# Softmax attention beside linear attention on one core: the last unit's normalisation, the range check, the head and the planner's keys are changed

## The chip, the cores and the metric

The kernel runs on one core of a Trainium2 chip. A core has a matrix engine (TensorE, PE in the profile), a vector engine (VectorE, DVE), an activation engine (ScalarE, ACT), a general engine (GpSimd, POOL), a queue engine that issues DMAs (SyncE, SP), an on-chip memory (SBUF) of 128 partitions and an accumulator memory (PSUM) of eight banks[...]. The metric is device time in microseconds (us), as the median of several executions.

## The reference: two attention layers whose outputs stand side by side

```python
qkv = (x @ wqkv).reshape(B, S, 3, H, Dh)          # B=1, S=2048, D=512, H=32, Dh=16; both layers
# A: softmax attention
p = softmax(einsum("bhqd,bhkd->bhqk", q, k) * Dh**-0.5)
a = einsum("bhqk,bhkd->bhqd", p, v).reshape(B, S, D) @ wo
# B: linear attention with a learned feature map
phi(t) = concat(softmax(t @ w_phi), softmax(-(t @ w_phi)))     # 32 features per head
kv = einsum("bhsf,bhsd->bhfd", phi(k), v);  z = phi(k).sum(over s)
b = (einsum(phi(q), kv) / (einsum(phi(q), z) + 1e-6)).reshape(B, S, D) @ wo
out = concatenate([a, b], axis=-1)                # [1, 2048, 1024], bf16
```

Nearly all the work is A's: 32 heads with a score matrix of 2048 x 2048 each.

## The kernel before

**A's tiling.** The work is cut into 32 units: a unit is a group g of four heads (eight groups, lined up two to a block of 128 projected columns, with a mask `hmask` that keeps every other head of the block in the key copy) and a chunk c of 512 queries. Each unit has 16 key tiles of 128 keys. For a key tile, PE makes four score blocks of 128 x 512 (`kq`, L654), one per head. They become exponentials in one of two ways. ACT applies exp to two or three blocks at once (L795, into `pT`). Or DVE makes them: it converts scores to 16-bit patterns that are read as floats (L852, into `rg`), and adds three shifts to the result (L873); the four versions are multiplied with four scaled copies of V, so the sum approximates exp. Of the 16 key tiles, five (`DK`) may go to DVE. PE multiplies all of them with V (L661) and collects a unit in one PSUM bank. V is stored as `VP` with 17 columns per head, the 17th being one, so that the row sums come along. PE also runs matmuls by zero (`filler`, L688) where its recent activity would fall too low.

**The end of a unit** (`make_unit_end`). DVE copies the bank to SBUF (`X`, L708). A DMA collects the row sums in `sums` (L714), DVE inverts them (L717), a DMA writes the inverses to HBM (`scr`, L720), four DMAs spread them over the partitions of `Yd` (L723), and POOL multiplies X by Yd in two halves (L730), into `OT` for an even group, into `Oo` for an odd one, from which four DMAs move it to its partitions of OT (L737). `X`, `Yd` and `Oo` have two buffers each. When the eight groups of a chunk are done, `out_proj` multiplies OT by wo (L918), DVE copies each of four row tiles to `OA` (L922), and a DMA stores it (L926).

**B** runs beneath A in steps that are released as A advances (`b_steps`): after its loads and the folding of w_phi into the weights, sixteen k-steps (L1002 to L1044) and sixteen q-steps. A q-step makes numerators and denominators on PE (L1078), divides by the feature sums on DVE (L1088, L1091), adds and normalises on POOL and DVE (L1105 to L1115), transposes on PE (L1121), copies the transposed tile on ACT (L1124), multiplies by wo (L1127), copies on DVE (L1131) and stores (L1134). Most of its buffers are double.

**The range check.** All this is valid only where sums lie in a range. After everything else, three DVE instructions count over `sums` and `rmin` (L1162 to L1166), two more combine the counts, a tiny matmul adds over partitions and DVE writes `flag` (L1172). A second program (`_general`) follows in the code; each engine loads the flag and skips it if the range holds.

**The order.** A planner (`_Sched`) writes each engine's instruction list when the program is built; on the chip each engine runs its list in order and waits on semaphores. Tasks stand in streams, one or more per engine, each with a weight from `_W`. `_choose` (L219) gives the head of each stream the start that the planner expects, adds the weight, and takes the lowest sum:

```python
st = self._start(t, r)
w = s["w"]
cand.append([st, st + (w(t) if callable(w) else w), s, r])
```

Here r is when the task's inputs and buffers are ready. The stream of score blocks for ACT, `pe_qa`, is `urgent`: other PE tasks that would delay it are charged `guard`. POOL's tasks wait for the last DVE task marked `port`. `b0`, `b1`, `b2` are the shares of A's key tiles at which B's k-steps begin, its q-steps begin, and they end; `p0`, `p1`, `p2` place the later Q and K projections; `cut` and `lead` say near the end of a unit when DVE may still take a tile.

**The head.** PE runs 16 warm-up matmuls (L536), then transposes the first 512 rows of x (L542). Copies of these go to `xT`; the first K projection, then the first Q projection follow (L581), then V row by row (L578).

## Time and profile before

The median of 14 executions is 798.89 us (794.47 to 801.3). The profiled execution took 800.21 us.

| | us |
|---|---|
| span of the profile | 798.4 |
| first exp on ACT starts | 12.60 |
| last exp on ACT ends | 760.48 |
| last copy of a B row tile (L1131) ends | 788.01 |
| last A row tile copied (L922) | 785.66 |
| flag written (L1172) ends | 790.38 |
| ACT busy | 752.3 |
| DVE busy | 722.1 |
| PE busy | 730.0 |

A line of the groups of instructions reads: line, engine, operation, output<-input, shapes, count | busy us, mean ns of one | idle us of the engine just before them, and what ended most of it. Mean durations overlap with the neighbours, so busy time divided by the count is what one costs in a row of them. A line of the stretches reads: from:to, its length, then busy us and number of instructions for each engine, then the granted PE clock (1 is full), the share of the DMA engines, and GB/s. The chain of waits gives start, length and instruction.

### The profile page before, as it was taken

To read this page: it belongs to the slowest core of one execution; us is meant where nothing else is said; L and a number is where in the kernel's file an instruction comes from. 1 tells how busy PE (TensorE), PEld (TensorE's weight loads), DVE (VectorE), ACT (ScalarE), POOL (GpSimd) and SP (SyncE) were. 2 spreads that over 40 slices of the span, in tenths; PEclk is the share of its full clock that TensorE was granted. 3 is DMA by queue.
4 is the path that set the end of the run, shared out by engine and by line. 5 is a ranking of instruction groups with operands and counts; after the bars stand their busy time and mean duration, and the time that the engine had idled before them with its cause. 6 is when DMAs were issued, how large, how long until landed. Compare 5 with 4: busy or idle time off the path is not lost.

```text
span 798.4 us, 17735 instructions
## 1 busy us (share of the span) xinstructions
PE 730.0 (91%) x7368; PEld 221.5 (28%) x7429; DVE 722.1 (90%) x1278; ACT 752.3 (94%) x819; POOL 157.5 (20%) x233
## 2 busy tenths in 40 slices
PE   8999999999998999899999899989999999999964
PEld 3322222232222232222222222222222222233331
DVE  1788999999998999999998989899999999978973
ACT  5999999999999999999998999999999999999930
POOL 5221111110003110000012322101103000164462
PEclk9999999999999999999997999999999999999987
DMA  7200000280000000000010000000000000000111
GB/s 146 66 9 8 7 6 13 50 183 8 13 32 15 9 4 11 9 12 9 18 29 9 12 2 12 9 9 12 9 25 20 20 10 12 8 15 18 28 44 52
DMA packets 44155, 19.62 MB, mean 25 GB/s; under 512 B 33312, under 2 KB 42016, under 8 KB 44064
## 3 DMA queue, kind: packets, MB, share of 16 engines
q1 hardware_dynamic: 42480, 17.60, 9.3%
q8 instruction: 60, 0.98, 0.5%
q10 hardware_dynamic: 1584, 0.79, 0.5%
q14 instruction: 31, 0.25, 0.1%
HBM read 7.88 MB, written 4.46 MB: 15 GB/s over the span
## 4 chain that ended last, share of the span: by engine, by line
ACT 83%; PE 11%; DVE 3%; issue 1%; DMA 0%; POOL 0%; DVEq 0%; ACTq 0%; POOLq 0%
ACT pT L795 78%; PE PS L654 3%; PE PS L661 3%; ACT e_k L1005 2%; PE PS L581 1%; ACT eT L1068 1%; DVE rg L852 1%; PE PS L536 1%; PE PS L1127 1%; ACT e_k L1124 1%; PE PS L578 1%; DVE rg L873 1%; PE PS L918 1%; ACT Wf L1068 0%; DMA out_dram<-e_k 0%
## 5 line engine op out<-in xcount | busy, mean ns | idle before, releaser
L795 ACT ACTIVATE pT<-PS 128x1024 bf16<-128x1024 f32 (+2 forms) x721 | 708.5, 1149 | 4.5 <-PE PS L654 4.3
L852 DVE TENSOR_SCALAR rg<-PS 128x512 uint16<-128x512 f32 x516 | 332.3, 683 | 17.8 <-PE PS L654 15.3
L654 PE MATMUL PS<-QT,KT 32*128 32x512 bf16 x2048 | 308.3, 387 | 31.9 <-ACT pT L795 26.7
L873 DVE TENSOR_SCALAR rg<-rg 128x2048 uint16<-128x2048 uint16 x387 | 251.8, 694 | 3.5 <-PE PS L661 3.0
L654 PEld LDWEIGHTS PS<-QT,KT 32*128 32x128 bf16 x2048 | 78.5, 91 | 292.1 <-ACT pT L795 230.3
L661 PE MATMUL PS<-pT,VP 128*32 128x512 bf16 x1532 | 153.1, 392 | 5.7 <-ACT pT L795 3.6
L661 PE MATMUL PS<-rg,VJ 128*32 128x512 f16 x1548 | 142.7, 388 | 0.4
L661 PEld LDWEIGHTS PS<-pT,VP 128*32 128x32 bf16 x1532 | 39.2, 93 | 97.8 <-issue 57.7
L730 POOL TENSOR_TENSOR Oo<-X,Yd 128x256 bf16<-128x256 f32 x32 | 22.8, 729 | 176.0 <-DVE rg L873 118.5
L730 POOL TENSOR_TENSOR OT<-X,Yd 128x256 bf16<-128x256 f32 x32 | 22.8, 728 | 171.6 <-DVE rg L873 136.8
L1015 POOL TENSOR_TENSOR w<-e_k,stat 128x512 bf16<-128x512 bf16 x32 | 33.7, 1073 | 100.7 <-DVE rg L873 46.8
L661 PEld LDWEIGHTS PS<-rg,VJ 128*32 128x32 bf16 x1548 | 39.2, 95 | 48.8 <-DVE rg L873 22.1
L661 PE MATMUL PS<-rg,VP 128*32 128x512 f16 x516 | 50.8, 384 | 0.2 <-DVE rg L852 0.2
L688 PE MATMUL PS<-ones_t,zer 128*32 128x512 bf16 x504 | 47.2, 388 | 0.0
L581 PE MATMUL PS<-xT,w 128*128 128x512 bf16 x114 | 34.0, 382 | 3.0 <-issue 1.9
L1105 POOL TENSOR_TENSOR w<-w 128x272 f32<-128x272 f32 x32 | 23.9, 762 | 41.7 <-DVE rg L873 29.6
L1124 ACT ACTIVATE e_k<-PS 128x512 bf16<-128x512 bf16 x16 | 10.3, 641 | 20.5 <-PE PS L1121 20.4
L708 DVE COPY X<-PS 128x512 f32<-128x512 f32 x32 | 21.9, 685 | 5.7 <-PE PS L661 5.6
L1091 DVE TENSOR_TENSOR w<-PS,stat 128x408 f32<-128x408 f32 (+1 forms) x48 | 25.2, 525 | 1.0
L1115 POOL TENSOR_TENSOR w<-w,den 128x256 bf16<-128x256 f32 x32 | 19.4, 622 | 28.0 <-DVE den L1111 9.4
L1127 PE MATMUL PS<-woB,e_k 128*128 128x512 bf16 x58 | 18.1, 415 | 2.9 <-ACT e_k L1124 1.0
L1008 DVE TENSOR_REDUCE stat<-e_k 128x64 f32<-128x1024 bf16 x16 | 19.5, 1216 | 0.7 <-ACT e_k L1005 0.4
(85 smaller groups left out, 425.0 us busy)
## 6 DMA issues: line engine op xcount, KB each, us to landing
Yd<-scr SPq DMA_DIRECT2D x128, 32.0 KB, 1.8
out_dram<-OA SPq DMA_DIRECT2D x16, 128.0 KB, 1.7
out_dram<-e_k SPq DMA_DIRECT2D x16, 128.0 KB, 1.7
OT<-Oo SPq DMA_DIRECT2D x64, 16.0 KB, 1.8
w<-in_A_wqkv_dram SPq DMA_DIRECT2D x2, 384.0 KB, 4.0
OT<-in_A_x_dram SPq DMA_DIRECT2D x1, 512.0 KB, 4.7
w<-in_A_wqkv_dram ACTq DMA_DIRECT2D x1, 512.0 KB, 7.9
WOp<-in_A_wo_dram SPq DMA_DIRECT2D x1, 512.0 KB, 6.4
```

The costliest lines, as they stand in the source:

```text
L581: return e.matmul(bank_of(t), w[:, ct, c0:c0 + 128], xT[:, ct, c * 512:(c + 1) * 512], start=(ct == 0), stop=(ct == 3))
L654: return e.matmul(out_ap, KT[32 * r:32 * r + n, g, kt * 128:(kt + 1) * 128], QT[32 * r:32 * r + n, c, g // 2, :], start=True, stop=True, t ...
L661: return e.matmul(PS[32 * r:32 * r + 32, pvb[u].idx, :], lhs(8 * (g // 2) + 2 * r + g % 2), rhs(r), start=t.res["first"], stop=t.res["last ...
L688: P.op("pe", lambda e, r=r: e.matmul(PS[32 * r:32 * r + 32, pvb[u].idx, :], zer[:], ones_t[:].unsqueeze(1).broadcast_to([128, 4, 128]), st ...
L730: ms.append(put(po_n, _Task("pool", 0.7, one("pool", lambda e, t, cs=cs: e.tensor_tensor(OT[:, c % 2, g // 2, cs] if even else Oo[:, ms[0] ...
L795: return e.activation(pT[:, p:p + n, :].rearrange("p a n -> p (a n)"), PS[:, b:b + n, :].rearrange("p a n -> p (a n)"), ACT.Exp, scale=0.25)
L852: return e.tensor_scalar(rg[:, q0.res["i"].idx, 512 * r:512 * r + 512], PS[:, qk.res["D"].idx, :], ya, yb, ALU.mult, ALU.add)
L873: ad = put(dv_ad, _Task("dve", 0.59, one("dve", lambda e, t, j=j: e.tensor_scalar(rg[:, t.res["j"].idx, :], rg[:, q0.res["i"].idx, :], flo ...
L1015: ph.append(put(po_phi, _Task("pool", 1.03, one("pool", lambda e, t, a=a: e.tensor_tensor(pk[ph[0].res["k"].idx][:, 512 * a:512 * a + 512] ...
L1091: muls.append(put(dv_y, _Task("dve", 0.485, one("dve", lambda e, t, yv=yv, lo=lo, n=n: e.tensor_tensor(ysv[r0.res["y"].idx][:, 136 * lo:13 ...
L1105: ad = [put(po_y, _Task("pool", 0.73, one("pool", lambda e, t, k=k: e.tensor_tensor(y3(0)[:, 2 * k:2 * k + 2], y3(0)[:, 2 * k:2 * k + 2], ...
L1127: o1, o2 = two_step(pe_o, lambda e, t, i: e.matmul(bank_of(t), oT_b[tp.res["t"].idx][:, i, :], woB[:, i, :], start=(i == 0), stop=(i == 3) ...
```

## The change

- **Last unit.** `last_unit` replaces the way over HBM for unit 31: PE multiplies X by a selection matrix `sel` in fp32, so that each head's row sums stand in all its partitions; DVE inverts them in four pieces of 128 columns from PSUM and multiplies each by X into `Oo`. The out-projection of the last chunk takes OT without the last odd group against `WOp` and `WOl[:, 0]`, and a fifth product of Oo against `WOl[:, 1]` is added per row tile; `WOl` is the last block of wo, with every other head's rows zeroed, made by POOL. The last row tile is copied by ACT. Unit 30 is multiplied by DVE in one piece.
- **All other units.** One DMA instead of four fills all partitions of Yd.
- **Range check.** It becomes planned tasks with two streams of their own (`dv_ck`, `pe_ck`), released at the last unit's X.
- **Head.** Q is projected first; K's first 128 keys are projected and copied alone, then the other 384 (`first_k`); 12 warm-ups instead of 16.
- **Planner.** A task's key falls by 0.03 per us that it has been ready; many weights, and b0, p1, p2, `cut`, are new.
- **B's oT copy** (L1124) goes to DVE. `VP` loses 16 spare columns, and its column of ones is filled in one instruction.

```diff
-                    cand.append([st, st + (w(t) if callable(w) else w), s, r])
+                    cand.append([st, st + (w(t) if callable(w) else w) - _W["age"] * (st - r), s, r])
...
-          dred=-0.1, dv=-0.081, dkv=-0.118, dy=-0.011, dd=-0.058, dob=-0.124, dmn=0.059, akf=-0.155,
-          aqf=-0.077, aot=-0.365, spare=9, early=0.0, guard=0.346, cut=4, lead=6, b0=0.315, b1=0.54, b2=0.99,
-          p0=8, p1=22, p2=5.753, lone=0, psh=0, pn=4, ps=-0.308, el=2, both=0)
+          dred=-0.076, dv=-0.053, dkv=-0.118, dy=-0.02, dd=0.003, dob=-0.124, dmn=0.059, akf=-0.019,
+          aqf=-0.072, aot=-0.365, age=0.03, early=0.0, guard=0.346, cut=5, lead=6, b0=0.286, b1=0.54, b2=0.99,
+          p0=8, p1=30, p2=6.012, psh=0, pn=1, ps=-0.308, el=2, both=0, va=16, ka=8, ota=0, xlat=3.6)
...
-    for i in range(16):
+    for i in range(12):
...
+    def first_k():
+        for lo, hi in ((0, 128), (128, 512)):
+            t0 = put(pe_pj, _Task("pe", 0.24 if hi == 128 else 0.65, pe_group(4, lambda e, t, ct, lo=lo, hi=hi: e.matmul(
+                PS[:, t.res["b"].idx, lo:hi], w[:, ct, 512:640], xT[:, ct, lo:hi], start=(ct == 0), stop=(ct == 3))),
+                [l_k0, xt_ready[(0, 0)], xt_ready[(0, 1)]], lat=PL, need=[("b", G, 1, 2)]))
...
-    proj("k", 0, 0, True)
     proj("q", 0, 0)
+    first_k()
...
+            if u == NU - 1:
+                col.append(d1)
+                last_unit(xv, xi, c)
+                range_check(xv, d1)
+                return
...
-            d3 = put(sp_q, _Task("sp", 2.0, dma(lambda t: d_s3[t.res["y"].idx], lambda e, t, r: e.dma_start(
-                Yd[32 * r + 16 * (g % 2):32 * r + 16 * (g % 2) + 16, t.res["y"].idx, :],
-                scr[u][r:r + 1, :].broadcast_to([16, 512])), 4), [d2], lat=2.2, need=[("y", y_sl, 1, 2)]))
+            d3 = put(sp_q, _Task("sp", 0.6, dma(lambda t: d_s3[t.res["y"].idx], lambda e, t, i: e.dma_start(
+                Yd[:, t.res["y"].idx, :], scr[u].unsqueeze(1).broadcast_to([4, 32, 512]))), [d2], lat=2.6,
+                need=[("y", y_sl, 1, 2)]))
...
+    def last_unit(xv, xi, c):
+        bc = put(pe_op, _Task("pe", 0.9, pe_group(1, lambda e, t, i: e.matmul(
+            PS[:, t.res["b"].idx, :], sel[:], X[:, xi, :], start=True, stop=True)), [xv], lat=PL, pre=[t_sel],
+            need=[("b", G, 1, 4)]))
+        parts = []
+        for k in range(4):
+            cs = slice(128 * k, 128 * k + 128)
+            r = put(dv_n, _Task("dve", 0.98, one("dve", lambda e, t, cs=cs: e.reciprocal(
+                Yd[:, parts[0][0].res["y"].idx if parts else t.res["y"].idx, cs], PS[:, bc.res["b"].idx, cs])), [bc], lat=DL,
...
+            m = put(dv_n, _Task("dve", 0.22, one("dve", lambda e, t, cs=cs: e.tensor_tensor(
...
-            te = put(ac_ot, _Task("act", 0.49, one("act", lambda e, t: e.activation(
...
+                te = put(dv_ot, _Task("dve", 0.35, one("dve", lambda e, t: e.tensor_copy(
...
-    c0 = P.op("dve", lambda e: e.tensor_scalar(
-        junk, sums[:], _A_LO, None, ALU.is_ge, ALU.add, accum_out=cnt[:, 0:1]), c_deps)
```

## The prediction

> **What bounds the kernel now.** I read the engine shares first, then the busy time in five stretches, then the chain of waits from the last exp to the end, then the groups of instructions behind each step.
>
> ```profile
> span 798.4 us, 17735 instructions
> PE 730.0 (91%) x7368; PEld 221.5 (28%) x7429; DVE 722.1 (90%) x1278; ACT 752.3 (94%) x819; POOL 157.5 (20%) x233
> ```
>
> Three engines look full. The stretches tell them apart:
>
> ```profile
> core 0: us, PE busy (x) PEld busy (x) DVE busy (x) ACT busy (x) POOL busy (x), PEclk, DMA share, GB/s
> 0.00:12.60 12.60, 10.62 (x49) 4.49 (x51) 2.46 (x4) 4.07 (x5) 9.66 (x28) 1.00 0.90 177
> 12.60:760.50 747.90, 699.46 (x7209) 208.28 (x7267) 698.89 (x1220) 742.72 (x806) 132.50 (x180) 0.99 0.09 21
> 760.50:788.40 27.90, 19.78 (x111) 8.69 (x110) 19.16 (x46) 5.53 (x10) 15.30 (x26) 0.82 0.19 60
> 788.40:790.40 2.00, 0.16 (x1) 0.08 (x1) 1.59 (x9) 0.00 (x0) 0.00 (x0) 1.00 0.21 70
> 790.40:798.40 8.00, 0.00 (x0) 0.00 (x0) 0.00 (x0) 0.00 (x0) 0.00 (x0) 0.59 0.05 13
> ```
>
> From the first exp (12.60) to the last (760.48) ACT is busy 742.7 of 747.9: ACT sets the pace. Then comes a tail of 28 us in which ACT does almost nothing, DVE works 19.2, the range check alone takes 2, and 8 us follow in which no engine works. Head, tail and check are 50 us without exps.
>
> ```profile
> L795 ACT ACTIVATE pT<-PS 128x1024 bf16<-128x1024 f32 (+2 forms) x721 | 708.5, 1149 | 4.5 <-PE PS L654 4.3
> L852 DVE TENSOR_SCALAR rg<-PS 128x512 uint16<-128x512 f32 x516 | 332.3, 683 | 17.8 <-PE PS L654 15.3
> L873 DVE TENSOR_SCALAR rg<-rg 128x2048 uint16<-128x2048 uint16 x387 | 251.8, 694 | 3.5 <-PE PS L661 3.0
> ```
>
> These are the attention tiles. DVE makes 516/4 = 129 of the 512 key tiles at (332.3+251.8)/129 = 4.53 us each, ACT the other 383 at 708.5/383 = 1.85 us. Together they make 1/1.85 + 1/4.53 = 0.761 tiles per us: an engine's us freed or lost is converted with these rates.
>
> The tail, by the chain of waits (start, length, what):
>
> ```profile
> 761.76 0.69 DVE X L708
> ...
> 764.11 3.44 DMA out_dram<-e_k
> ...
> 777.81 1.89 PE PS L1127 x4
> 779.70 4.03 PE PS L918 x14
> 783.74 0.05 issue
> 783.79 0.38 PE PS L918
> 784.17 0.24 PE PS L1121 x4
> 784.43 0.61 ACT e_k L1124
> ```
>
> Two chains share it. A's last unit: X copied at 762.45, its multiply on POOL at 772.00, out-projection L918 at 779.5, last A copy L922 done at 785.66. B's q-steps: eight of the sixteen casts L1131 fall after 763, the last ends at 788.01. They hold each other up: transposes L1121 of B stand behind L918 on PE, and out_dram<-e_k behind the last unit's DMAs on SP. B is late because it was starved: POOL's L1115 is busy 0.9 us in 617 to 697 and 6.2 us in 697 to 730, while DVE's L852 fills the first stretch.
>
> **What the Trainium skill says.** "FP8 and Floating Point Precision", TensorE Precision Notes: a true FP32 matmul takes four passes. No fp32 matmul is in this trace; four warm 512-column passes at the 0.216 us spacing seen here give an estimate of 0.86 us. "TensorE: Matmul & The Clock Gate", Part 1: the clock is released by a busy window of about 3.4 us that runs freely; Part 4: transposes do not count as busy. The trace agrees so far: warm-up matmuls come 0.43 us apart until about 6.6 us, then at half that. "SBUF — State Buffer", Summary: a DVE instruction in a two-port mode, or with two SBUF inputs against POOL's reads, blocks POOL for its length. POOL's longest waits here are for L873, 137 and 119 us before L730.
>
> **The change part by part.** The sum is made in span; the profiled run took 800.21 (span 798.4 plus 1.8), 1.3 above the median 798.89, from which I subtract.
>
> *Head.* Four warm-ups fewer at 0.43 us: the queue would empty at 6.2, the transposes start at 7.12 now, and x has landed at 0.79 + 4.7 = 5.5, so 0.9 us gain. If the clock is still low, 16 transposes at twice 0.055 lose 0.9 and eight projection matmuls at 0.21 more lose 1.7: a loss of 1.7 is the other end. I take 0. Q before K, and K for 128 keys alone: today Q's cast ends at 11.88 and ACT takes two K copies (10.39 to 11.65) and a V copy before the exp at 12.60. With Q's four matmuls first (9.3 to 10.2), four of 128 columns (0.25) and a short K copy, the exp can start at about 11.4: 1.2 gained; two more copies on ACT lose about 0.4. The V load (issued 1.9, lands after 7.9) covers the V matmuls from 10 on. POOL's ones (8.2 us, becoming one strided fill), the 16 columns less of VP and two WOl multiplies stay under POOL's first awaited work at 17.5 and its 80% idle. **Head −1.0 (−2.5 to +1.5).**
>
> *oT copy from ACT to DVE.* Ten of sixteen L1124 lie in the body, 0.49 us each in the chain: ACT gains 4.9. On DVE I take 0.40 (L556 copies twice the elements from PSUM in 0.69; bounds 0.35 and 0.69): DVE loses 4.0. That is 4.9/1.85 − 4.0/4.53 = 1.77 tiles, or **−2.3** (−1.4 to −2.6).
>
> *Range check.* Now L1162 to L1172, ending at 790.38, 2.0 after the last output issue on SP (788.37). Done earlier on DVE, **−2.0**; its 1.8 us of DVE work go into the tail below. Uncovered it costs all 2.0 again.
>
> *Last unit.* Removed: one small reciprocal, 1 + 4 + 4 DMAs (their issues on SP: 1.17, 1.71 and 2.47 us), and two POOL multiplies. Added: one fp32 matmul (0.9, twice that at the low clock), four reciprocals of 128 columns from PSUM (L1088: 295 ns for 24 columns, 235 for 16, so about 7 ns each more: 1.0 us; L1011's 547 for 64 says 0.95) and four multiplies (272 columns take 426, so 0.3): 5.2 us on DVE. A's chain from X (762.45) becomes 1.1 + 0.2 + 5.2, the last product and copy 1.1, issue 0.35: 10 us after the last exp against 25.5 now. The first three products per row tile are ahead of it. The single Yd DMA of the other units shortens SP's issue from 1.7 to about 0.5 and doubles the bytes to 256 KB; a unit lasts 23 us and X has two buffers, so it is hidden.
>
> *The tail as a sum.* DVE's 19.2 us hold X 0.69, a reciprocal 0.24 and four A copies 2.75; 15.5 are B. After, with B as late as now: 15.5 + six oT copies 2.4 + X 0.7 + three A copies 2.1 + chain 5.2 + check 1.8 = 27.7, which fills today's 27.9. So removing DMAs alone brings nothing: DVE is late next. The gain must come from B's backlog.
>
> *Age and the new weights.* Each us that a ready task waits lowers its key by 0.03. A B multiply (about −0.02) passes an A conversion (−0.165) after 5 us; today it never does while conversions are ready. Raising the A adds from 0.031 to 0.113 and starting k-steps at 0.286 instead of 0.315 (22 us) push the same way. One us of B on DVE moved into the body costs 0.221/0.761 = 0.29 us there and gives 1/0.9 in the tail (nine tenths packed). I take 12 of the 17.9 us (B with its oT copies): the tail is 15.7/0.9 = 17.4, −10.5 + 3.5 = **−7.0**. Bounds: all but 2 moved, a tail of 13 us (A's own 10 and some waits), −10.2; none moved, 27.7/0.9 = 30.8, +2.9.
>
> Sum: −1.0 − 2.3 − 2.0 − 7.0 = −12.3; 798.89 − 12.3 = **786.6**. That is 780 to 793 within this case.
>
> **The rivals.**
> *Backlog stays, DVE bounds the tail.* The reciprocals and oT copies stand in DVE's queue before B: −1.0 − 2.3 − 2.0 + 2.9 = −2.4, **796.5**. For: the sum above; against: the starving in 617 to 697 is what age acts on.
> *Better packing.* DVE idles 49 us in the body, mostly unnamed gaps and waits on L654. With B as steady filler and 2% less idle, 15 us of DVE make 3.3 tiles, 4.3 us more: with the full backlog moved, −1.0 − 2.3 − 2.0 − 10.2 − 4.3 gives **779**.
> *Slower: age delays ACT's feed.* PE is 93% busy in the body. There are some 390 groups of B, projection and out-projection matmuls; an old one of 0.43 us may now be placed ahead of a QK group, and ACT waits with everything behind it. It decides from 12.3/390 = 32 ns of ACT idle per group; at 45 ns, +5 and **804**. Against: ACT has waited only 4.3 us for L654, two score banks lie ahead of it, and the guard of 0.346 stays.
> That the broadcast does nothing is the first rival: B's end at 788.01 already stood after A's 785.66.
>
> **How the numbers follow.** Backlog drains 0.66, stays 0.14, better packing 0.11, ACT starved 0.09. A measurement can tell about 0.3% (2.4 us, below 796.5 and above 801.3). Faster: 0.66 + 0.11 + half of 0.14 = 0.84; same 0.06; slower 0.10. The range of 776 to 797 leaves out the starved case, part of the second and the end of the third, about 0.18.
>
> **What would show it.** First exp near 11.4; L1124 gone from ACT; last flag write before the last output issue; L1115 spread evenly over 600 to 760 and three or four L1131 casts after the last exp; last exp to last issue 17 us; DVE tiles a few fewer than 129. Wrong if the 8 us at the end grow, if eight casts still follow the last exp, if ACT's idle before L795 rises above 12 us, or if matmuls stay at half speed past 9 us.

## The result and the profile after

The changed kernel takes 790.45 us (median of 10 executions, 779.57 to 795.59) against 797.86 (47 executions, 793.24 to 802.46) of the kernel before, measured beside it. The ratio of 0.984 (95% interval 0.980 to 0.987) leaves out, as all ratios below do, executions that lay over 1.5% above the fastest of their kernel, five of the changed kernel's, and so flatters the change somewhat: with all of them in, and at the same granted clock, it is 0.988 (787.6 against 797.3, see the table of the experiments). 786.6 was forecast, with 776 to 797 as its range. The profiled execution took 789.63 us, its span is 787.9.

The engine shares of the changed kernel:

```profile
span 787.9 us, 17366 instructions
PE 727.3 (92%) x7249; PEld 218.5 (28%) x7331; DVE 716.3 (91%) x1275; ACT 754.2 (96%) x818; POOL 154.7 (20%) x218
```

Its stretches (head, body, tail, end), with the columns that the prediction's table has:

```profile
0.00:10.11 10.11, 8.19 (x44) 3.73 (x44) 2.46 (x4) 3.40 (x6) 4.17 (x15) 1.00 0.93 191
10.11:769.75 759.64, 712.98 (x7181) 212.41 (x7260) 705.74 (x1248) 749.08 (x811) 150.52 (x203) 0.98 0.10 27
769.75:782.10 12.35, 6.13 (x26) 2.36 (x27) 8.14 (x23) 1.69 (x4) 0.00 (x0) 1.00 0.07 23
782.10:787.90 5.80, 0.00 (x0) 0.00 (x0) 0.00 (x0) 0.00 (x0) 0.00 (x0) 0.62 0.20 59
```

The first exp starts at 10.11 and the last ends at 769.75; the last issue is at 782.1. Against before:

| stretch | before | after | difference | forecast |
|---|---|---|---|---|
| to the first exp | 12.60 | 10.11 | −2.5 | −1.0 |
| first to last exp (body) | 747.9 | 759.6 | +11.8 | +1.2 (oT −2.3, B moved in +3.5) |
| last exp to last issue or flag (tail) | 29.9 | 12.35 | −17.6 | −12.5 (B −10.5, check −2.0) |
| no engine works, to the end | 8.0 | 5.8 | −2.2 | 0 |
| span | 798.4 | 787.9 | −10.5 | −12.3 |

The sum is close to the forecast, and its terms are not: the tail fell by 5 us more, and the body grew by ten times what I had given it. The groups that make the tiles, after:

```profile
L894 ACT ACTIVATE pT<-PS 128x1024 bf16<-128x1024 f32 (+1 forms) x731 | 716.4, 1125 | 9.9 <-PE PS L690 9.8
L951 DVE TENSOR_SCALAR rg<-PS 128x512 uint16<-128x512 f32 x500 | 325.0, 683 | 24.5 <-PE PS L690 21.6
L972 DVE TENSOR_SCALAR rg<-rg 128x2048 uint16<-128x2048 uint16 x375 | 250.1, 703 | 3.4 <-PE PS L697 3.1
```

L894 is the exp, L951 the convert, L690 and L697 the two attention matmuls (L795, L852, L654, L661 before). DVE makes 500/4 = 125 tiles instead of 129, so ACT has 16 blocks more. ACT's idle time ahead of the exps doubled, 4.5 to 9.9, all of it a wait for L690; DVE's wait for L690 rose from 15.3 to 21.6. A DVE tile costs (325.0 + 250.1)/125 = 4.60 instead of 4.53.

With the two stretch tables the body's growth can be added up (it is bookkeeping: the parts have to make up the whole, and it says what was longer, not why). A microsecond of ACT is worth (1/1.85)/0.761 = 0.71 us of body, one of DVE (1/4.53)/0.761 = 0.29. DVE work that is no tile: 698.9 − 584.1 = 114.8 before, 705.7 − 575.1 = 130.6 after, +15.8, worth +4.6: this is B and its oT copies. ACT work that is no exp: 34.2 before, 32.7 after, −1.1. ACT's idle in the body: 5.2 before, 10.6 after, +3.8. DVE's idle: 49.0 before, 53.9 after, +1.4. Dearer DVE tiles: 125 x 0.07 = 8.8, +2.5. Together +11.2 of the 11.8.

Not all of this is the change. In the profile of before PE ran 13.7 us of the body at half its clock, in that of the changed kernel 23.9. The run a_oldlast below has the changed body, with the same instructions in the same order on ACT, DVE and POOL, and 13.7 us at half clock:

```profile
10.32:765.92 755.60, 708.28 (x7181) 211.43 (x7260) 705.58 (x1248) 748.56 (x811) 149.13 (x203) 0.99 0.10 28
```

Against the body of before this is +7.7: DVE's work +4.7 and ACT's −1.2 as above, dearer DVE tiles +2.5, but ACT's idle only +1.3 (7.0 instead of 5.2 us) and DVE's +0.3. Most of the idle time in the sum above goes with the clock of that execution.

The tail by the chain of waits of the changed kernel (L697 the last attention matmul, L744 X, L832 the range check, L799 and L802 the inverses and multiplies, L809 and L815 the out-projection, L1025 and L1029 the copies of row tiles on ACT and DVE):

```profile
768.27 1.49 ACT pT L894
769.76 0.04 issue
769.81 0.43 PE PS L697 x4
770.24 0.02 issue
770.26 0.70 DVE X L744
...
772.38 0.88 DVE Yd L799
...
776.88 1.04 PE PS L809 x4
777.92 0.23 PE PS L815
...
779.28 1.71 DMA out_dram<-OA
```

No B line is left in it: no cast of B follows the last exp, where eight did. A's chain alone sets the end, and the forecast had it right in kind: X, four inverses with the multiplies between them (772.38 to 776.84, 4.5 us), the last products, the copies.

### The profile page after: what moved, and what is told of

It is laid out like the page before. It is cut to its first block, busy times and chain, and to the rows that moved or that the text cites. A ratio compares the mean times of both kernels' runs of the same rounds, so it can differ in the third digit from the quotient of the medians.

```text
span 787.9 us, 17366 instructions
## 1 busy us (share of the span) xinstructions
PE 727.3 (92%) x7249; PEld 218.5 (28%) x7331; DVE 716.3 (91%) x1275; ACT 754.2 (96%) x818; POOL 154.7 (20%) x218
## 4 chain that ended last, share of the span: by engine, by line
ACT 83%; PE 9%; DVE 4%; DMA 2%; issue 0%; POOL 0%; SPq 0%; POOLq 0%
ACT pT L894 79%; PE PS L690 3%; PE PS L697 2%; ACT e_k L1111 2%; ACT eT L1174 1%; DVE rg L951 1%; PE PS L588 1%; DVE rg L972 1%; DMA sums<-X 1%; DMA Yd<-scr 1%; PE PS L543 1%; DVE Wf L1096 1%; PE PS L591 0%; DVE Yd L799 0%; PE PS L1108 0%
## 5 line engine op out<-in xcount | busy, mean ns | idle before, releaser
L894 ACT ACTIVATE pT<-PS 128x1024 bf16<-128x1024 f32 (+1 forms) x731 | 716.4, 1125 | 9.9 <-PE PS L690 9.8
L951 DVE TENSOR_SCALAR rg<-PS 128x512 uint16<-128x512 f32 x500 | 325.0, 683 | 24.5 <-PE PS L690 21.6
L690 PE MATMUL PS<-QT,KT 32*128 32x512 bf16 x2048 | 314.9, 388 | 24.3 <-ACT pT L894 18.9
L972 DVE TENSOR_SCALAR rg<-rg 128x2048 uint16<-128x2048 uint16 x375 | 250.1, 703 | 3.4 <-PE PS L697 3.1
L697 PE MATMUL PS<-pT,VP 128*32 128x512 bf16 x1548 | 155.3, 393 | 6.5 <-ACT pT L894 3.6
L690 PEld LDWEIGHTS PS<-QT,KT 32*128 32x128 bf16 x2048 | 79.2, 91 | 287.0 <-ACT pT L894 215.7
L697 PE MATMUL PS<-rg,VJ 128*32 128x512 f16 x1500 | 138.8, 389 | 0.8 <-DVE rg L972 0.6
L697 PEld LDWEIGHTS PS<-pT,VP 128*32 128x32 bf16 x1548 | 40.2, 94 | 91.0 <-issue 47.3
L697 PEld LDWEIGHTS PS<-rg,VJ 128*32 128x32 bf16 x1500 | 37.7, 95 | 57.4 <-issue 27.0
L697 PE MATMUL PS<-rg,VP 128*32 128x512 f16 x500 | 49.9, 390 | 0.2 <-DVE rg L951 0.2
L776 POOL TENSOR_TENSOR Oo<-X,Yd 128x256 bf16<-128x256 f32 x30 | 25.0, 850 | 95.1 <-DMA Yd<-scr 61.0
L724 PE MATMUL PS<-ones_t,zer 128*32 128x512 bf16 x448 | 40.7, 386 | 0.0
L591 PE MATMUL PS<-xT,w 128*128 128x512 bf16 x109 | 32.0, 382 | 3.7 <-issue 1.5
L744 DVE COPY X<-PS 128x512 f32<-128x512 f32 x32 | 21.9, 683 | 3.4 <-PE PS L697 3.3
L627 POOL TENSOR_SCALAR KT<-KT,hmask 128x512 bf16<-128x512 bf16 x12 | 8.3, 692 | 77.4 <-DVE KT L601 47.8
L1108 PE MATMUL PS<-Wf,xT 128*128 128x512 bf16 x52 | 17.6, 413 | 2.1 <-issue 1.4
```

Of the source, the lines that this page charges most:

```text
L591: return e.matmul(bank_of(t), w[:, ct, c0:c0 + 128], xT[:, ct, c * 512:(c + 1) * 512], start=(ct == 0), stop=(ct == 3))
L690: return e.matmul(out_ap, KT[32 * r:32 * r + n, g, kt * 128:(kt + 1) * 128], QT[32 * r:32 * r + n, c, g // 2, :], start=True, stop=True, t ...
L697: return e.matmul(PS[32 * r:32 * r + 32, pvb[u].idx, :], lhs(8 * (g // 2) + 2 * r + g % 2), rhs(r), start=t.res["first"], stop=t.res["last ...
L724: P.op("pe", lambda e, r=r: e.matmul(PS[32 * r:32 * r + 32, pvb[u].idx, :], zer[:], ones_t[:].unsqueeze(1).broadcast_to([128, 4, 128]), st ...
L744: xv = _Task("dve", 0.61, one("dve", lambda e, t: e.tensor_copy(X[:, t.res["x"].idx, :], PS[:, pvb[u].idx, :])), [], lat=DL, need=[("x", x ...
L776: ms.append(put(po_n, _Task("pool", 0.7, one("pool", lambda e, t, cs=cs: e.tensor_tensor(OT[:, c % 2, g // 2, cs] if even else Oo[:, ms[0] ...
```

## The experiments

Every execution also lists its mean granted clock of PE, and within each kernel the time follows it nearly in a line, mostly by 0.5 to 0.7 us per 0.001 (95 executions of the kernel before, from 0.976 to 0.994: 0.52). Medians of a few executions therefore differ by 3 us and more with the clock. So I also read each kernel's time at a clock of 0.985 from a straight line through its own executions; the ± is the standard error of that line.

| kernel | executions | median us | ratio to before, 95% | mean clock | us at 0.985 |
|---|---|---|---|---|---|
| before | 95 | 798.2 | 1 | 0.984 | 797.3 ± 0.1 |
| changed | 12 | 789.5 | 0.984 [0.980, 0.987] | 0.983 | 787.6 ± 0.3 |
| a_age0 | 20 | 795.95 | 0.996 [0.994, 0.999] | 0.982 | 794.2 ± 0.3 |
| b_age | 4 | 805.4 | 1.012 [1.003, 1.020] | 0.969 | 796.7 ± 2.3 |
| b_weights | 5 | 805.6 | 1.009 [1.006, 1.012] | 0.980 | 802.2 ± 0.8 |
| b_last | 20 | 804.1 | 1.008 [1.005, 1.011] | 0.984 | 802.7 ± 0.2 |
| a_oldlast | 12 | 798.2 | 1.001 [0.998, 1.004] | 0.975 | 792.8 ± 0.7 |
| a_ota1 | 11 | 791.5 | 0.992 [0.989, 0.995] | 0.989 | 792.8 ± 0.4 |
| a_check_end | 20 | 789.4 | 0.989 [0.987, 0.992] | 0.982 | 788.6 ± 0.3 |
| a_warm16 | 10 | 786.7 | 0.986 [0.982, 0.990] | 0.988 | 788.0 ± 0.3 |
| a_oldhead | 4 | 788.75 | 0.988 [0.984, 0.992] | 0.992 | about 792.7 |
| a_tail | 4 | 782.3 | 0.983 [0.979, 0.986] | 0.987 | 784.3 ± 0.4 |
| a_tail2 | 6 | 789.7 | 0.988 [0.983, 0.993] | 0.979 | 784.6 ± 0.7 |
| a_force | 4 | 851.7 | 1.066 [1.060, 1.072] | 0.989 | 853.8 ± 0.5 |

(The changed kernel's row has two executions more than the comparison above, its interval is of that comparison. a_oldhead's four executions all lie at 0.992; its last figure is an estimate with 0.55 us per 0.001, the middle of the other slopes.)

Two things limit the last column. First, part of a time can lie outside the profiled span: time minus span is 1.7 to 1.9 us in most kernels, but on average 3.0 in b_last, 2.6 in a_oldhead, 2.5 in a_ota1 and 2.1 in b_age. So 1.2 us of what b_last is slower than before, and 0.7 to 0.8 of what a_ota1 and a_oldhead are slower than the changed kernel, is no work of the engines; what it is stays open.

Second, an equal mean clock is not an equal clock where it costs time. Up to the last exp, ACT, DVE and POOL run the same instructions in the same order in six of the profiles:

| profile | us of the body at half clock | body, us |
|---|---|---|
| a_warm16 | 10.2 | 754.4 |
| a_oldlast | 13.7 | 755.6 |
| a_check_end | 20.5 | 757.7 |
| changed | 23.9 | 759.6 |
| a_tail | 27.3 | 760.0 |
| a_tail2 | 30.7 | 761.3 |

They lie on a line to 0.6 us: 751.0, and 0.34 us for each us at half clock. In the tails of a_oldlast, b_age and b_weights another 13.7 us lie at half clock, but there PE mostly waits (in a_oldlast it is busy for 2.7 of them, so they can cost 1.3 us at most). They lower the mean clock as much as in the body, and so the last column makes these three look better than they are, by some 2.5 to 4.6 us (an estimate: 13.7 times 0.34, less what they can cost). In the profile of before 10.2 us of the tail lie at half clock, with PE busy for 7.2 of them, in the changed kernel's none. So at an equal clock in the body the change is worth 10 to 14 us (an estimate: 9.7, and up to 10.2 times 0.34, and 0.7 for the end without work). Whether the change itself brings more half clock into the body (four of the six profiles have more than the 13.7 us of before) is open.

### What drains B: age, the weights, or the rest?

**a_age0**, the changed kernel with the age term at zero:

```diff
-          aqf=-0.072, aot=-0.365, age=0.03, early=0.0, guard=0.346, cut=5, lead=6, b0=0.286, b1=0.54, b2=0.99,
+          aqf=-0.072, aot=-0.365, age=0.0, early=0.0, guard=0.346, cut=5, lead=6, b0=0.286, b1=0.54, b2=0.99,
```

> The changed kernel with the age term at 0, all else as changed. Theory (the age term drains B's backlog): B's q-steps are starved again; three or more of the sixteen casts of B's row tiles fall after the last exp, the stretch from the last exp to the last output issue grows from 12.3 us to 20 us or more, and the time is 794 to 799 us. Rival (the new weights, the earlier k-steps and the oT copy on DVE do it alone): at most one cast after the last exp and a time within 3 us of 790.5.

The tail is the same without age: last exp 775.72, last issue 788.06, 12.3 us, no cast of B in it; POOL's normalisation of B is spread as in the changed kernel. My theory fell. Age is worth 6.6 us at an equal clock all the same, but in the body (765.4 us instead of 759.6): without it DVE makes 123 tiles instead of 125, 8 blocks more for ACT or 8 x 1.85/4 = 3.7 us, DVE idles 62.9 us instead of 53.9, ACT's idle ahead of the exps is 11.3 instead of 9.9. Its body has 20.5 us at half clock, no more than the changed kernel's.

**b_age**, the kernel before with the age term alone:

```diff
-                    cand.append([st, st + (w(t) if callable(w) else w), s, r])
+                    cand.append([st, st + (w(t) if callable(w) else w) - 0.03 * (st - r), s, r])
```

> The kernel before with nothing but the age term of 0.03 in the planner's key. Theory: B is spread (POOL's normalising of B busy 3 us or more between 617 and 697 us instead of 0.9, at most three casts of B after the last exp); what then ends the kernel is A's last unit with its 25.5 us from the last exp to its last issue, so 792 to 796 us against 797.9. Rival (age delays the matmuls that feed ACT): ACT's idle before its exps above 12 us and a time above 799 us.

No cast of B after the last exp either, and a tail of 21.95: A's old chain. So age is able to drain B, but the changed kernel doesn't need it. The last exp moved from 760.5 to 775.3, and the gain was gone; ACT's idle ahead of the exps rose from 4.5 to 10.3. A clock of 0.969, the lowest of all kernels, is in that (30.7 us of the body at half clock instead of 13.7), and with four executions the time at an equal clock says no more than "not faster by much".

**b_weights**, the kernel before with the new weights and no age:

```diff
...
-          aqf=-0.077, aot=-0.365, spare=9, early=0.0, guard=0.346, cut=4, lead=6, b0=0.315, b1=0.54, b2=0.99,
-          p0=8, p1=22, p2=5.753, lone=0, psh=0, pn=4, ps=-0.308, el=2, both=0)
+          aqf=-0.072, aot=-0.365, lone=0, spare=9, early=0.0, guard=0.346, cut=5, lead=6, b0=0.286, b1=0.54, b2=0.99,
+          p0=8, p1=30, p2=6.012, psh=0, pn=1, ps=-0.308, el=2, both=0, va=16, ka=8, ota=0, xlat=3.6)
```

> The kernel before, with only the new weights of the planner and no age term. B's backlog was gone from the tail with age alone and also in the changed kernel without age, so something else drains it as well. Theory: the new weights do (k-steps from 0.286, cheaper B multiplies on the vector engine, dearer A adds). Then at most two casts of B follow the last exp, and the tail from the last exp is 20 to 23 us, the old chain of A's last unit; time 790 to 795 at the clock of the kernel before. Rival: it is the rest of the change, the oT copies that leave ACT and the short last unit, which shift the plan; then six to eight casts still follow, the tail stays at 28 to 31 us, and the time is 796 to 801.

The theory's half about the plan holds: no cast after the last exp, a tail of 22.4. Its half about the time fails: the kernel is slower than before by 4.9 us at an equal clock. The stretches of b_weights, body and tail:

```profile
12.44:777.55 765.11, 728.09 (x7287) 214.33 (x7285) 698.82 (x1231) 755.92 (x829) 145.53 (x203) 0.99 0.09 22
777.55:799.95 22.40, 6.27 (x21) 2.16 (x21) 5.69 (x15) 0.00 (x0) 1.40 (x2) 0.70 0.11 33
```

The body is 17.2 us longer than before, for a tail that is 7.5 shorter. DVE is busy for as long as before (698.8 and 698.9), though it now does all of B: it makes 125 tiles instead of 129. And it is idle for 66.3 us instead of 49.0, ACT for 9.2 instead of 5.2. With the rates above, the DVE idle time is 5.0 us of the 17.2 and ACT's 2.8; DVE's extra work that is no tile (131.1 − 114.8) is 4.7 and ACT's 2.3 (six oT copies and three eT exps more). Some 2.3 us of this are the clock's (20.5 us of the body at half clock instead of 13.7). Work moved out of the tail was not laid into holes of the body; the engines idle more than before.

### What is the broadcast worth?

**b_last**, the kernel before with the last unit by broadcast and its out-projection; the check stays at the end, VP loses its spare columns to make room:

```diff
...
+            if u == NU - 1:
+                col.append(d1)
+                last_unit(xv, xi, c)
+                return
...
```

> The kernel before with the last unit normalised over TensorE and its out-projection in the new form (to have room for the two new tensors, V's 16 spare columns are left out as in the change); the range check stays at the end. Theory of the prediction (DVE bounds the tail as long as B is late): 796 to 799.5 us, no change. Rival (A's chain sets the end of the tail): 10 us less, 786 to 790 us.

Neither came: it made the kernel slower, by 5.4 us at an equal clock, of which 4.2 lie within the span. The body is unchanged (747.0), the tail has grown from 29.9 to 37.0. Its chain of waits shows how (L775 the four first products per row tile, L781 the fifth, L1182 B's multiplication by wo, L1186 B's cast, L1217 the check):

```profile
769.18 4.45 PE PS L775 x10
...
773.85 0.57 PE PS L775
774.42 0.23 PE PS L781
...
775.81 1.92 PE PS L1182 x8
...
791.32 1.90 PE PS L1182 x4
793.25 0.69 DVE e_k L1186
```

One cast of B, at 764.7, comes after the last exp, and then none for 12 us. DVE has no work for 5.70 of these, as its own timeline says:

```profile
776.89 0.69 DVE L1186 CAST e_k<-PS 128x512 bf16<-128x512 f32 x1 [5.70 <-PE PS L1182]
```

PE's list has the sixteen first products ahead of B's; from 767.4 to 774.2 they run at half clock, which draws this out. (In the profile of before 10.2 us of the tail are at half clock, here 6.8.) A is done sooner than before and B, which set the end anyway, later. DVE is busy 22.9 of the 37.0 us: it isn't full, B's steps stand one behind another.

**a_oldlast**, the changed kernel with the old way over HBM for the last unit; the check stays in the plan, under that unit:

```diff
-                col.append(d1)
-                last_unit(xv, xi, c)
                 range_check(xv, d1)
-                return
...
```

> The changed kernel with the last unit normalised by the old way over memory and POOL, and with the old out-projection; the rest of its order is as changed, the range check included. Theory (with B finished, A's own chain is all that is left in the tail): from the last exp to the last output issue 24 to 27 us instead of 12.3, so 801 to 806 us. Rival (the old chain hides under what else is in the tail): at most 4 us more than 790.5.

The tail is 21.9 us (24 to 27 was expected) instead of 12.3, and at an equal mean clock the kernel is 5.2 us slower. That is too little by what was said above: 13.7 us of this run's half clock lie in its tail. Its body, 755.6, is on the line of the changed kernel's, so at an equal clock in the body the difference of the two profiles is the tail's 9.6 us, of which at most 1.3 goes with the half clock there. With B drained A's chain is the end, and shortening it counts. So what the broadcast is worth changes its sign with B, here at an equal mean clock:

| | old last unit | broadcast |
|---|---|---|
| B late (kernel before, b_last) | 797.3 | 802.7 |
| B drained, and all other parts of the change (a_oldlast, changed) | 792.8 | 787.6 |

The rows differ in more than B: the second has the new head, the oT copy on DVE and the planned check too. Draining B alone (b_age, b_weights) gives 797 to 802: nothing that could be told, or a loss. Draining and the broadcast without the other parts was not run.

### The other parts

**a_ota1**, the changed kernel with B's oT copy back on ACT:

```diff
-          p0=8, p1=30, p2=6.012, psh=0, pn=1, ps=-0.308, el=2, both=0, va=16, ka=8, ota=0, xlat=3.6)
+          p0=8, p1=30, p2=6.012, psh=0, pn=1, ps=-0.308, el=2, both=0, va=16, ka=8, ota=1, xlat=3.6)
```

> The changed kernel with B's oT copy on ACT again. Theory of the prediction (16 copies of 0.49 us in a full ACT against 16 of 0.42 on DVE, exchanged at the rates of the two engines): 2.3 to 3.7 us slower at the same clock, about 793 us. Rival (B's chain waits for ACT behind exps again, B is late in the tail): 6 us slower or more, with casts of B after the last exp.

At an equal clock 5.2 us slower. With B drained all sixteen copies lie in the body: 16 x 0.49 = 7.8 us of ACT are worth 5.6, 16 x 0.42 = 6.8 of DVE 2.0, net 3.6; 0.7 more lies outside the span (above), and 0.9 is not explained by the counts, though DVE did take 127 tiles instead of 125. The profiled executions alone (788.4 at a clock of 0.988, 787.9 at 0.982) would have shown a difference of 0.5.

**a_check_end**, the changed kernel with the range check after everything else, as before:

```diff
-                range_check(xv, d1)
                 return
...
```

> The changed kernel with the range check after everything else, in the form of the kernel before; all other instructions stay in their order. Theory of the prediction: the last DVE instruction comes 2.0 us after the last output issue, 2.0 us slower. Rival A (the stores of the last rows are still on their way for 1.7 us, so the check is hidden behind their landing): less than 0.5 us. Rival B (the 1.3 us of check between the last unit's copy and its first inverse are in the way now and go away): 1 us slower or less. And if the 2.2 us that the end without engine work has become shorter (5.8 against 8.0) hang on where the flag is written, the end grows to 8 here, 4 us slower in all.

The flag is written 2.0 us after the last issue (782.01 against 779.99), and the tail is 14.3 against 12.35. In the times it is 1.0 ± 0.4; its profile has 3.4 us more at half clock after the last exp, and whether the missing 1 us is in that is open. The idle time at the end is 5.8 as in the changed kernel, so the flag's place isn't what shortened it, and the check isn't hidden behind the landing of the last stores (rival A). Nor is the planned check in the way of the first inverse (rival B): from the start of X to that inverse it takes 1.91 us here and 2.03 with the check in between, as DVE waits 1.22 us for the broadcast here.

**a_warm16**, the changed kernel with sixteen warm-up matmuls:

```diff
-    for i in range(12):
+    for i in range(16):
```

> The changed kernel with 16 warm-up matmuls again; every other instruction is the same, in the same order. Theory (PE's queue of warm-ups held the transposes back, and all that follows moves with them): the first exp starts 1.6 us later (11.7 instead of 10.1) and the whole kernel ends 1.6 us later at the same granted clock: 791 to 793 us. Rival (the V load or the planner's order takes the head start back): first exp at 11.7, but no difference beyond 0.5 us at the end.

No difference that could be told at an equal clock (788.0 ± 0.3 and 787.6 ± 0.3); the theory's 1.6 us would have shown. In its profile the first exp is at 10.25, not at 11.7: PE's transposes start at 5.84, with twelve warm-ups at 5.70. The sixteen took 4.96 us, because the clock was granted at 3.8 us there, at 5.2 in the changed kernel's profile and 6.8 in that of before. "TensorE: Matmul & The Clock Gate", Part 1, of the Trainium skill says that the window runs freely and that the length of the warm-up varies between runs of one kernel; these profiles agree.

**a_oldhead**, the changed kernel with K first and no lone key tile:

```diff
+    proj("k", 0, 0, True)
     proj("q", 0, 0)
-    first_k()
```

> The changed kernel, but K is projected before Q again, for all 512 keys, without the lone key tile. First theory: order and lone tile gave about 1.5 of the 2.5 us by which the first exp came earlier (the four warm-up matmuls gave nothing). Then the first exp is at 11.4 to 11.8 instead of 10.1, and the time 1.2 to 1.7 us longer at an equal clock. Rival: the first exp moves, but what follows waits for the V load and for the other K columns anyway; then the exps of the first 40 us end within 0.5 us of the changed kernel's and the time is longer by less than 0.5 us. The planner places everything after it anew, so 1 us of packing is uncertain in both.

The first exp is at 11.61, 1.5 later. Not all of it is the order: in this profile the clock was granted at 6.5 instead of 5.2, and the transposes start at 6.14 instead of 5.70, the first four of them at half clock. From the first transpose to the first exp it takes 5.5 us (5.3 in the kernel before) instead of 4.4. By 60, 100, 150 and 200 us ACT and DVE have made 110, 228, 371 and 518 blocks of scores, in the changed kernel 117, 230, 377 and 522: four blocks are a tile, 1/0.761 = 1.3 us, so about this much of the head start is kept. The time at an equal clock is longer by about 5, more than either theory says; 0.8 of it lies outside the span. The planner placed all that follows anew: DVE makes 124 tiles instead of 125. The head is at most 1.5 of the 5; the rest belongs to the plan that came with it.

**a_force**, the changed kernel with many more filler matmuls:

```diff
-    ACTIVE = 0.60
-    FORCE = 0.40
+    ACTIVE = 0.85
+    FORCE = 0.55
```

> The changed kernel with more filler matmuls: the planner must keep TensorE active 0.85 of each 3.42 us window, up to a filler of 0.55, instead of 0.60 and 0.40. First theory: the stretches at half clock follow thin windows of TensorE; more filler keeps the mean granted clock of the runs at 0.990 or above, and they spread less than the 0.973 to 0.996 of the changed kernel. Rival: the stretches come whatever TensorE does; the mean clock stays at 0.980 to 0.986 with the same spread, and the time follows it. The order changes widely, so the time itself may differ by 5 us either way and only the clock is read.

The mean clock is 0.989 (0.984 to 0.995): between the two expectations, so it settles nothing about the clock; nor did the edit take away the thin windows of PE (see the last section). What it shows is the price of PE's time. Fillers and exps of a_force:

```profile
L724 PE MATMUL PS<-ones_t,zer 128*32 128x512 bf16 x1488 | 147.0, 392 | 0.0
L894 ACT ACTIVATE pT<-PS 128x1024 bf16<-128x1024 f32 (+1 forms) x753 | 729.8, 1091 | 52.3 <-PE PS L690 28.6 <-PE PS L697 22.3
```

The fillers take 147 us of PE (448 of them in a_tail2 took 41), ACT's idle rises to 52 us, and the kernel is 66 us longer at an equal clock. Of 106 us more on PE, 66 come through: PE has little slack here, it is the next bound behind ACT and DVE.

### A version that is faster still

**a_tail** is the changed kernel with three edits after the last exp: the broadcast goes to a score bank, so that the fourth group of first products no longer waits 2.16 us for its bank; the last two row tiles get output buffers of their own out of `pT`; their copies alternate between ACT and DVE.

```diff
-            need=[("b", G, 1, 4)]))
+            need=[("b", A_bank, 1, 4)]))
...
-            out_rows(c, st, f, t, st % 4 != 3)
+            out_rows(c, st, f, t, st % 2 == 0)
...
+        sl, buf, ds = (pt_sl, pT, [d_ox[st % 2]] * NPT) if c == 3 and st > 1 else (oa_sl, OA, d_oa)
```

> The changed kernel with a shorter end: the broadcast sum lies in a score bank that is free by then, so that no row tile's products wait for its bank; two more output buffers (unused exp tiles), so that no copy waits for a store; copies of the row tiles alternate between DVE and ACT. The body is the same, instruction by instruction. Theory (in the 12.3 us after the last exp, 2.2 us are PE's wait for the bank and 1.7 a copy's wait for a store): the tail shrinks to 8.5 to 9.5 us and the kernel is 3 us faster at the same clock, 786 to 788. Rival (four inverses and multiplies on DVE are the whole chain, and the two waits hide behind them): less than 1 us.

> The same kernel as a_tail, timed again in more rounds: the broadcast into a score bank, two more output buffers, output copies on DVE and ACT in turn. Theory: its body is the changed kernel's instruction by instruction and only the tail is shorter, by 2.2 us to the last issue; time 784.3 at a clock of 0.985 against 787.6, ratio to the kernel before 0.982 to 0.985. Rival: the four times so far were luck with the clock; then it is within 1 us of the changed kernel at an equal clock, ratio 0.987 to 0.989.

Its chain of waits at the end (the two runs are of the same kernel; this is a_tail's):

```profile
769.98 0.43 PE PS L697 x4
...
771.18 1.13 PE PS L793 x2
...
772.36 3.40 PE PS L809 x15
...
778.79 0.69 DVE pT L1029
...
780.21 0.15 DVE flag L840
```

The last exp ends at 769.93 and the last issue is at 779.84: 9.9 us instead of 12.3. The flag now ends later, at 780.36, so the work is done 10.4 us after the last exp, 1.9 sooner. At an equal clock the two runs give 784.3 ± 0.4 and 784.6 ± 0.7, 3.1 below the changed kernel, though the medians (782.3 and 789.7) lie on either side of it, and a_tail2's ratio, 0.988, is what its rival said: the clock was 0.987 in the one and 0.979 in the other. About 1 of the 3.1 us is not accounted for by the tail.

## Why the prediction was right, point by point

The time fell into the range, 4 us above the figure, and the likeliest case, "backlog drains", is what happened to the tail. Several terms of its sum were wrong and cancelled: that the figure came so close is in good part luck, that the change is faster and that the tail is where it gains is not.

*Head, −1.0; measured −2.5.* (Its parts, −1.2 and +0.4, make −0.8, and the transposes of before start at 7.33, not at 7.12.) The step "the exp can start at about 11.4: 1.2 gained" was right in size: from the first transpose to the first exp it takes 4.4 us instead of 5.3, so order and lone tile are worth 0.9. The other 1.6 is the transposes' start, 5.70 instead of 7.33. Fewer warm-ups and the time at which the clock was granted (5.2 instead of 6.8) both enter it, and one profile of each can't part them; over the executions of a_warm16 the warm-ups are worth 0.5 ± 0.4, so the 0 taken for them is neither confirmed nor far off.

*oT copy, −2.3 (−1.4 to −2.6); about −5.2 measured, −4.7 of it in the span.* The cost on DVE (0.40 taken, 0.42 measured) was right. The term "ten of sixteen lie in the body" was mis-sized: I counted where the copies lay before, and the same change brings all sixteen into the body. Sixteen give −3.6.

*Range check, −2.0; −1.0 ± 0.4 in the times, −1.9 in the tail.* Within the change the check's two long counts stand ahead of the first inverse (L832 ends at 772.37), but under the broadcast, and cost 0.1 us there.

*Last unit.* The pieces were sized well: an inverse 1.0 taken, 0.95 alone and 0.88 in the chain measured; a multiply 0.3 and 0.29; four of each 5.2 and 4.9 (772.29 to 777.15); the broadcast 0.9 taken, from four passes, and 1.1 measured. "10 us after the last exp" was 12.3, and the step that failed is "the last product and copy 1.1, issue 0.35": from the last multiply to the last issue it takes 4.9 us. The fourth row tile waits for its bank and two copies wait for an output buffer; a_tail takes these waits away, and its last issue comes 2.4 sooner. The sum of the tail also has three A copies on DVE: it is ACT that copies three of the last four row tiles, and DVE the fourth, 1.4 us less. The step "removing DMAs alone brings nothing" was too kind: −1.0 − 2.3 − 2.0 + 2.9 had this part at +2.9 with the check in it, b_last shows +5.4. "DVE is late next" was the wrong engine to name: DVE idled 5.7 us in one piece there, and B's chain through PE's list was late.

*Age and the weights, −7.0 (tail −10.5, body +3.5).* This step failed twice.
First, its cause. "A B multiply passes an A conversion after 5 us" isn't why the tail emptied: without age it is as empty (a_age0), with the weights alone too (b_weights). Age and the weights are each sufficient. Which of the weights does it was not tried; the k-steps' start b0 and the dearer A adds are both candidates, and only argued.
Second, its price. I took 12 of 17.9 us of B moved, and none is left in the tail; and I priced the body by work alone, 0.29 us per us of DVE. At that price the 15.8 us of DVE work that the body gained come to 4.6, but dearer DVE tiles (+2.5) and idle time were left out: ACT +3.8 and DVE +1.4 in the profile of the change, of which all but 1.6 goes with 10.2 us more at half clock (a_oldlast has the same body without them). In b_weights idle time alone is 7.8, some 2.3 of it the clock's. Why the DVE tiles are dearer was not looked into.

*End, 0; −2.2 measured.* The idle time after the last work is 8.0 before, 7.6 in b_weights, 6.9 in b_age, and 5.5 to 6.3 in all others, b_last among them, which has the old check. The cause stays open.

*The rivals.* "Backlog stays" is refuted for the change, and realised by b_last. "Better packing" had the full drain right and the packing wrong: DVE's idle rose. "Age delays ACT's feed" has the sign of age wrong in the changed kernel: it is worth 6.6 us, and without it ACT waits longer. Added alone to the kernel before, age came with 10.3 us of ACT's idle instead of 4.5, in part the clock's; there the rival is not refuted.

*What would show it.* Met: L1124 gone from ACT, the flag before the last issue (779.27, 782.07), POOL's normalisation spread over 560 to 770 (3.64, 3.64, 2.40, 2.40 us in the four stretches 560, 620, 680, 730 to 770), 125 DVE tiles, ACT's idle at 9.9. Not met: the first exp near 11.4, which was at 10.1; three or four casts and 17 us of tail; it was none and 12.3.

## What to carry to other kernels

Two chains that share a tail are one problem: shortening A's alone gave +5.4 us, emptying the tail of B alone 0 to +5, and in the kernel where both are done the short chain is worth 5 to 10 (5.2 at an equal mean clock, 8.3 to 9.6 by stretch). So they are to be changed, priced and measured together. Work moved from a tail into a full body costs more than its own time at the body's rates: here 4.7 us for the work, 2.5 for dearer tiles of the engine that took it and 1.6 for idle time, at the same time at half clock; it is to be read from the stretch, not from the work moved. Before comparing kernels that differ by less than one per cent, look at the granted clock of each execution: here 0.01 of it was 5 to 7 us, more than most of the parts. And look at where it fell: 13.7 us at half clock cost 4.6 us in the full body, and at most 1.3 in a tail in which PE waits.

## What the runs showed of the hardware

The clock falls to half in the middle of a kernel whose PE is nearly always at work. In the fourteen profiles 33 such stretches begin between the first and the last exp, ten of 3.41 us, seven of 6.83, thirteen of 10.24 and three of 13.65. In the changed kernel's profile there are three, from 251, 319 and 606. Windows of 3.41 us ahead of them, the last one always right before the fall, and the first stretch:

```profile
240.75:244.17 3.42, 3.39 (x27) 0.81 (x26) 3.33 (x8) 3.42 (x5) 1.05 (x1) 1.00 0.03 2
244.17:247.58 3.41, 3.25 (x56) 1.28 (x56) 3.36 (x6) 3.41 (x5) 0.00 (x0) 1.00 0.23 79
247.58:250.99 3.41, 2.83 (x48) 0.93 (x44) 3.40 (x7) 3.41 (x5) 1.45 (x3) 1.00 0.05 7
250.99:261.23 10.24, 9.75 (x74) 2.08 (x72) 6.35 (x13) 8.02 (x9) 3.44 (x4) 0.50 0.08 28
312.43:315.85 3.42, 3.26 (x31) 0.93 (x28) 3.42 (x7) 3.42 (x4) 0.00 (x0) 1.00 0.07 15
315.85:319.26 3.41, 2.53 (x55) 1.01 (x51) 3.31 (x8) 3.41 (x5) 2.07 (x2) 1.00 0.00 0
599.15:602.57 3.42, 3.19 (x29) 0.82 (x28) 3.30 (x7) 3.42 (x6) 2.90 (x3) 1.00 0.00 0
602.57:605.98 3.41, 1.96 (x17) 0.44 (x17) 3.03 (x6) 3.41 (x4) 1.55 (x4) 1.00 0.08 19
```

DVE and ACT, which had been all but full, are busy 6.35 and 8.02 of the 10.24 us at half clock, as they wait for scores. In the window right before each fall PE is busy 2.83, 2.53 and 1.96 of 3.41 us, that is 0.83, 0.74 and 0.57, against 0.92 over the whole span. The same can be counted in all profiles, as the clock's changes within one lie whole multiples of 3.41 us apart. The 33 windows right before a fall have PE busy 0.51 to 0.89, 0.74 in the middle. Of the windows at full clock with less than 0.7, 11 of 18 are followed by a fall; of the 2423 with 0.9 or more, none is. (Ten of the profiles lack some matmul records and can show a window too thin; the four with as many matmuls as weight loads give 0.56 to 0.89 before their ten falls.) So every fall here follows a window thinner than the average, though not every thin window brings one; that the thin window causes it is not shown. More filler (a_force) was meant to test that and didn't: its windows right before its two falls are still at 0.57 and 0.73. "TensorE: Matmul & The Clock Gate", "Why this matters for your kernels", of the Trainium skill ties mid-kernel drops to idle gaps of PE of some 3 us; the longest gap in these bodies is 1.93 us, 1.44 in the changed kernel's, so that rule doesn't cover this case.

A stretch of 10.24 us is 0.0064 of the mean clock and costs about 3.5 us in the body (0.34 each, above). One of 10.24 lies in the tail of before, from 771, and may cost less there.

An fp32 matmul of 512 columns takes 1.1 us in two records (L793). An inverse of 128 columns from PSUM takes 0.95 us, three times a multiply of the same columns.
